# Loading an output projection in two halves of sixteen heads instead of five pieces, in a one-core decode kernel on Trainium2

## The chip, the cores and the metric

The kernel runs on one core of a Trainium2 chip. The metric is the device time of one launch in microseconds (us). A run with rounds is timed in turn with the kernel before on the same chip.

The engines in the profile: PE is TensorE's matmul, PEld its weight load, DVE is VectorE, ACT ScalarE, POOL GpSimd, and SP the SyncE engine, which issues the loads. A q behind an engine's name means its sequencer, which waits, branches and issues (PEq, SPq). L860 means line 860 of that kernel's source. A packet is one record of the DMA engines' work; in these wo loads it is one contiguous row of one partition (the 10 KB part below has 128 packets of 10,240 bytes). A load with one row per partition is thus eight packets for each of the 16 DMA engines.

## The reference

One decode step: attention of 32 query heads over 8 key/value groups with a cache of 65,536 keys, plus a feed-forward branch, both added to x.

```python
q = (x @ wq).reshape(1, 1, 32, 128).transpose(0, 2, 1, 3)
k = jnp.repeat(k_cache, 4, axis=1)          # [1, 8, 65536, 128] -> 32 heads
v = jnp.repeat(v_cache, 4, axis=1)
p = softmax(einsum("bhqd,bhkd->bhqk", q, k) * 128 ** -0.5)
o = einsum("bhqk,bhkd->bhqd", p, v)
A = o.transpose(0, 2, 1, 3).reshape(1, 1, 4096) @ wo      # wo: [4096, 512]
B = gelu(xn @ w1 + b1) @ w2 + b2            # xn = layernorm(x), also A's input
return x + A + B
```

The two caches are 268 MB of the 280.5 MB that the kernel reads. wo is 4 MB, 32 KB for each of the 128 partitions, and it is the last thing loaded.

## The kernel before

K, V and finally wo come through one queue (SP's) into one large SBUF buffer. A piece of wo goes over the place of the last but one K block. The last V block lands before wo, and while wo comes in, the last attention output is finished and weighted.

A piece of wo is loaded with contiguous rows per partition: with `(p r) n -> p r n`, partition p holds wo rows p*r to p*r + r - 1. These rows mix heads and elements, so the attention output of a piece must be spread to the same order. Before, seven groups of four heads were loaded in pieces of 16, 8 and 4 heads (4, 2 and 1 groups, WP), and spread. The eighth group was loaded head by head (1 KB rows), so its output needed no spreading.

```python
def dma_wo():
    for i, (g0, n) in enumerate(WP):              # 16, 8, 4 heads
        r = n * HPG                               # HPG = 4 heads of a group
        sch.dma(SP, lambda ...: sp.dma_start(
            out=wo_sb[:, g0 * HPG:g0 * HPG + r, :],
            in_=A_wo[g0 * HPG * DH:(g0 + n) * HPG * DH, :].rearrange("(p r) n -> p r n", r=r)),
            wsem[i], writes=[f"wo{i}"])
    for i, n in enumerate((3, 1)):                # the last group: 3 heads and 1
        ... in_=A_wo[...].rearrange("(h p) n -> p h n", p=128) ...
```

Spreading is a VectorE multiplication of the output (oT_all) by a 0/1 mask (part_m) into oM_bf. Placing is a TensorE product of oM_bf with a second mask (part_r), then a cast to oX_bf. The final sum is 32 rows of four products, each row one of a partition's 32 rows of wo:

```python
for i, (g0, n) in enumerate(WP):                  # place: three products, one cast
    sch.op(PE, lambda ...: pe.matmul(pA[:, PA_O + g0 * HPG:PA_O + g0 * HPG + r],
                                     lhsT=oM_bf[:, i, :], rhs=part_r[i][:, :], ...))
sch.op(DVX, lambda: dve.tensor_copy(out=oX_bf[:, :], in_=pA[:, PA_O:PA_O + GE * HPG]), ...)
weigh_3(GE, G, "oL")                              # the last group's output
...
for i, (g0, n) in enumerate(WP):
    for r in range(g0 * HPG, (g0 + n) * HPG):
        for kt in range(KT):                      # KT = 4 column strips
            fin_mm(kt, oX_bf[:, r:r + 1], wo_sb[:, r, kt * 128:(kt + 1) * 128], ["oX", f"wo{i}"], ...)
for h in range(HPG):                              # the last group
    ... fin_mm(kt, oT_all[...], wl_sb[:, h, ...], ["oL", f"wl{0 if h < WH[0] else 1}"], ...)
```

The kernel's outer block, with its loop over the K and V blocks, ends behind the first 64 of these products; all engines meet there.

Of the kernel before, what the change touches and what calls it, by code (L numbers as in the profile page):

```python
# [6 lines left out]
BF = mybir.dt.bfloat16  # L7
F32 = mybir.dt.float32
ACTF = mybir.ActivationFunctionType
ALU = mybir.AluOpType  # L10
AX = mybir.AxisListType
# [229 lines left out]
def bass_parallel_sum__gqa_block_cached__dense_activation_gelu__decode_kernel(  # L241
# [13 lines left out]
    D = A_x.shape[-1]  # L255
    DH = 128
    H = A_wq.shape[1] // DH
    G = A_k_cache.shape[1]
    HPG = H // G
# [3 lines left out]
    KT = D // 128  # L263
    TPF = 8
    FPU = 16
    TPD = FPU * TPF
# [20 lines left out]
    sch = _Sched(nc)  # L287
    PE = sch.add_engine("pe", "pe", is_pe=True)
    DVE = sch.add_engine("dve", "dve")
    ACT = sch.add_engine("act", "act")  # L290
    POOL = sch.add_engine("pool", "pool")
    SP = sch.add_engine("sp", "sp")
    DVX = sch.add_engine("dvx", "dvx")
# [3 lines left out]
    pe = nc.tensor  # L297
    dve = nc.vector
    act = nc.scalar
    pool = nc.gpsimd  # L300
    sp = nc.sync

    def sb(name, shape, dt):
        return nc.alloc_sbuf_tensor(name, shape, dt)

    ident_bf = sb("ident_bf", [128, 128], BF)
    ident_f = sb("ident_f", [128, 128], F32)
# [5 lines left out]
    kv = sb("kv", [128, 3 * PCOL], BF)  # L313
    at_k1 = kv_at = nc.sbuf_base - 6 * PCOL
    late = [kv_at + 40 * 1024]
    early = [at_k1 + 2 * PCOL]

    def sb_in(place, name, shape, dt):
        t = nc.alloc_sbuf_tensor_at(name, shape, dt, offset=place[0])
        n = (4 if dt == F32 else 2) * math.prod(shape[1:])  # L320
        place[0] += (n + 31) // 32 * 32
        return t
# [23 lines left out]
    w2_at = w1_at + KT * F  # L346
    w2_sb = kv[:, w2_at:w2_at + FC * D].rearrange("p (fc n) -> p fc n", fc=FC)
    GE = G - 1
    WP = []
    g0 = 0  # L350
    while g0 < GE:
        n = next(m for m in (4, 2, 1) if g0 + m <= GE)
        WP.append((g0, n))
        g0 += n
    wo_sb = kv[:, 0:GE * HPG * D].rearrange("p (r n) -> p r n", n=D)
    wl_at = TPD * DH
    wl_sb = kv[:, wl_at:wl_at + HPG * D].rearrange("p (h n) -> p h n", h=HPG)
    kt_ring = sb("kt_ring", [128, NKT * FCOL], BF)
    P_bf = [sb(f"P_bf{i}", [128, CW], BF) for i in range(2)]
    P_v = [P_bf[i][:, :].rearrange("p (t j) -> p t j", j=HPG) for i in range(2)]  # L360
# [15 lines left out]
    rden = sb_in(late, "rden", [128, H], F32)  # L376
    o_sum = sb_in(late, "o_sum", [128, H], F32)
    oT_all = sb_in(late, "oT_all", [128, H], BF)
    oX_bf = sb_in(late, "oX_bf", [128, GE * HPG], BF)
    oM_bf = sb_in(late, "oM_bf", [128, len(WP), 128], BF)  # L380
    part_m = [sb(f"part_m{i}", [128, DH // (n * HPG)], BF) for i, (_, n) in enumerate(WP)]
    part_r = [sb(f"part_r{i}", [128, n * HPG], BF) for i, (_, n) in enumerate(WP)]
    flag = sb("flag", [1, 2 * NU], BF)

    pst = [nc.alloc_psum_tensor(f"pst{i}", [128, 1024], BF) for i in range(NPT)]
# [1 line left out]
    pA = nc.alloc_psum_tensor("pA", [128, 512], F32)  # L387
    pO = nc.alloc_psum_tensor("pO", [128, 512], F32)
# [4 lines left out]
    PA_O = 64  # L393
    PA_ST = 128
    PO_SUM = HPG

    csem = [sch.dsem(f"csem{i}") for i in range(6)]
    sem_x = sch.dsem("dx")
    sem_misc = sch.dsem("dmisc")
    sem_w1 = sch.dsem("dw1")  # L400
    sem_w2 = sch.dsem("dw2")
    wsem = [sch.dsem(f"wsem{i}") for i in range(len(WP))]
    lsem = [sch.dsem(f"lsem{i}") for i in range(2)]
    sem_out = sch.dsem("dout")

    for t, res in ((ident_bf, "ident_bf"), (ident_f, "ident_f")):
# [4 lines left out]
                out=t[:, :], in_=t[:, :], compare_op=ALU.not_equal, fill=1.0,  # L411
                base=0, pattern=[[-1, 128]], channel_multiplier=1,
            ),
            reads=[res], writes=[res],
# [62 lines left out]
        sch.dma(SP, lambda: sp.dma_start(out=w2_sb, in_=B_w2.rearrange("(p fc) n -> p fc n", fc=FC)),  # L477
                sem_w2, writes=["w2"])

    WH = (HPG - 1, 1)  # L480

    def dma_wo():
        for i, (g0, n) in enumerate(WP):
            r = n * HPG
            sch.dma(SP, lambda g0=g0, n=n, r=r: sp.dma_start(
                out=wo_sb[:, g0 * HPG:g0 * HPG + r, :],
                in_=A_wo[g0 * HPG * DH:(g0 + n) * HPG * DH, :].rearrange("(p r) n -> p r n", r=r)),
                wsem[i], writes=[f"wo{i}"])
        h0 = 0
        for i, n in enumerate(WH):  # L490
            sch.dma(SP, lambda h0=h0, n=n: sp.dma_start(
                out=wl_sb[:, h0:h0 + n, :],
                in_=A_wo[(H - HPG + h0) * DH:(H - HPG + h0 + n) * DH, :].rearrange("(h p) n -> p h n", p=128)),
                lsem[i], writes=[f"wl{i}"])
            h0 += n

    dma_small()
    dma_wq()
# [262 lines left out]
    def weigh_3(a, b, res):  # L761
        cs, hs = slice(a * GW, b * GW), slice(a * HPG, b * HPG)
        sch.op(DVX, lambda: dve.tensor_tensor(out=o_c[:, cs], in0=o_all[:, cs], in1=coef[:, cs], op=ALU.mult),
               reads=["coef", "o0", "o1"], writes=["o_c"])
        sch.op(DVX, lambda: dve.tensor_reduce(out=heads(o_sum, a, b), in_=by_head(o_c, a, b), axis=AX.X,
                                              op=ALU.add), reads=["o_c"], writes=["o_sum"])
        sch.op(DVX, lambda: dve.tensor_tensor(out=oT_all[:, hs], in0=o_sum[:, hs], in1=rden[:, hs], op=ALU.mult),
               reads=["o_sum", "rden"], writes=[res])


    def spread():
        for i, (g0, n) in enumerate(WP):
            r, a = n * HPG, DH // (n * HPG)
            sch.op(DVX, lambda g0=g0, n=n, i=i, r=r, a=a: dve.tensor_tensor(
                out=oM_bf[:, i, :].rearrange("p (h a) -> p h a", a=a),
                in0=oT_all[:, g0 * HPG:g0 * HPG + r].unsqueeze(2).to_broadcast([128, r, a]),
                in1=part_m[i][:, :].unsqueeze(1).to_broadcast([128, r, a]), op=ALU.mult),
                reads=["oT", f"part_m{i}"], writes=[f"oM{i}"])


    def body(i):
        last = i == NU // 2 - 1
        for f in range(2 * FPU):
            transposes(i, f)
            if f == 1:
                load_q(i)
            if f % FPU == FPU - 1:
                done_chunk(f"K{i % 2}{'ab'[f // FPU]}")
            if f == FPU + LAG + 1:
                stats_1()  # L790
            if f == FPU + LAG + 3:
                stats_2(2 * i)
            if f in W_AT:
                weights(2 * i, W_AT.index(f))
            if f >= LAG:
                scores(f - LAG)
        for f in range(2 * FPU - LAG, 2 * FPU):
            scores(f)
        pv(2 * i, 0, 24)
        stats_1()  # L800
        pv(2 * i, 24, 48)
        stats_2(2 * i + 1)
        for j in range(HPG):
            weights(2 * i + 1, j)
        keep_max(i)
        if last:
            weigh_1()
        pv(2 * i, 48, TPD)
        pv(2 * i + 1, 0, 32)
        total(i)  # L810
        if last:
            weigh_2()
            weigh_3(0, GE, "oT")
            spread()
        pv(2 * i + 1, 32, TPD)

    W_AT = [FPU + LAG + 4 + 2 * j for j in range(HPG)]
# [10 lines left out]
        sch.reads.setdefault(res, []).append(made)  # L828
    free.update(("K1a", "K1b", "Va", "Vb"))
    issue_chunks()  # L830
    for i, (_, n) in enumerate(WP):
        r = n * HPG
        for t, res, pat in ((part_m[i], f"part_m{i}", "p (a r) -> p a r"), (part_r[i], f"part_r{i}", "p (a r) -> p r a")):
            sch.op(DVE, lambda t=t, pat=pat, r=r: dve.tensor_reduce(
                out=t[:, :], in_=ident_f[:, :].rearrange(pat, r=r), axis=AX.X, op=ALU.max),
                reads=["ident_f"], writes=[res])
    marks, marks2 = [], []
    for i in range(NU // 2):
        marks.append(len(PE.ops))
# [5 lines left out]
    marks.append(len(PE.ops))  # L845


    for i, (g0, n) in enumerate(WP):
        r = n * HPG
        sch.op(PE, lambda g0=g0, i=i, r=r: pe.matmul(  # L850
            pA[:, PA_O + g0 * HPG:PA_O + g0 * HPG + r], lhsT=oM_bf[:, i, :], rhs=part_r[i][:, :], start=True, stop=True),
            reads=[f"oM{i}", f"part_r{i}"], writes=["pA"])
    sch.op(DVX, lambda: dve.tensor_copy(out=oX_bf[:, :], in_=pA[:, PA_O:PA_O + GE * HPG]), reads=["pA"], writes=["oX"])
    weigh_3(GE, G, "oL")

    R = 0
    pR = pss[R]

    def fin_mm(kt, lhsT, rhs, reads, first, last, publish):
        sch.op(PE, lambda: pe.matmul(pR[32 * kt:32 * kt + 1, 0:128], lhsT=lhsT, rhs=rhs, start=first, stop=last),  # L860
               reads=reads, writes=[f"pss{R}"], publish=publish)

    for kt in range(KT):
        fin_mm(kt, ones_f[:, 0:1], f_rows[:, kt * 128:(kt + 1) * 128], ["f_rows", "ones_f"], True, False, kt == KT - 1)
    rest = {}
    for i, (g0, n) in enumerate(WP):
        if i == 1:
            rest.update((e, len(e.ops)) for e in (PE, DVE, SP))
        for r in range(g0 * HPG, (g0 + n) * HPG):
            for kt in range(KT):  # L870
                fin_mm(kt, oX_bf[:, r:r + 1], wo_sb[:, r, kt * 128:(kt + 1) * 128], ["oX", f"wo{i}"], False, False,
                       r == (g0 + n) * HPG - 1 and kt == KT - 1)
    for h in range(HPG):
        for kt in range(KT):
            fin_mm(kt, oT_all[:, GE * HPG + h:GE * HPG + h + 1], wl_sb[:, h, kt * 128:(kt + 1) * 128],
                   ["oL", f"wl{0 if h < WH[0] else 1}"], False, h == HPG - 1, h == HPG - 1 and kt == KT - 1)
    NR = 32 * (KT - 1) + 1
    sch.op(DVE, lambda: dve.tensor_copy(out=fin_bf[0:NR, :], in_=pR[0:NR, 0:128]),
           reads=[f"pss{R}"], writes=["fin"])
# [3 lines left out]
        sem_out, reads=["fin"], writes=["out_dram"],  # L883
# [5 lines left out]
    n = len(head)  # L889
# [61 lines left out]
```

## Time and profile before

| | before |
|---|---|
| time, median of 3 runs | 656.14 us (655.99 to 656.57) |
| span of the profiled run | 654.7 us |
| DMA packets of SP's queue (q1) | 6744 |
| granted TensorE clock, mean, and in the windows from 641 us on | 0.786, and 0.50 |
| last V block lands | 642.21 us |
| last piece of wo lands | 652.20 us |
| TensorE's last product ends | 652.61 us |

A landing is the start of the DMA's issue plus its time "from issue to landing". It is read to 0.01 us, so sums can be off by 0.01. The last column of an issue line is that time, the column before it the size. In a timeline line the columns are start, length, engine, line and operation, output and inputs, shapes, count, and in brackets the idle time just before with what ended it. The lines themselves are shown in the prediction.

### The profile page before, as it was taken

How to read it: one execution, taken by the hardware profiler on the slowest of the kernel's cores; microseconds unless marked ns; L12 is line 12 of the kernel's file. 1: busy time of each engine (PE TensorE's matmuls, PEld its weight loads, DVE VectorE, ACT ScalarE, POOL GpSimd, SP SyncE). 2: the span in 40 equal slices, each digit the busy share in tenths (PEclk: the TensorE clock that was granted, in tenths of full speed). 3: DMA queues.
4: the chain of work that ended last, by engine and by line, in shares of the span. 5: the costliest groups of instructions: out<-in, count | busy, mean ns of one | idle time of the engine just before them, and what ended most of it. 6: DMA issues, size and time to landing. Idle time of an engine off the chain costs nothing.

```text
span 654.7 us, 29020 instructions
## 1 busy us (share of the span) xinstructions
PE 532.5 (81%) x12682; PEld 506.2 (77%) x12682; DVE 281.6 (43%) x574; ACT 249.9 (38%) x454; POOL 5.6 (1%) x74
## 2 busy tenths in 40 slices
PE   2388498696969959697895969879596996998997
PEld 0187498696969959697895969879596996998996
DVE  3245063361625436162552616345261633645363
ACT  0134053351624425153451615335161543535351
POOL 0000000000000000000000000000000000000000
PEclk9789598695968869596895959679595877969695
DMA  9999999999999999999999999999999999999997
GB/s 385 444 428 438 419 447 434 436 424 444 436 424 424 444 436 428 424 444 440 420 436 433 440 424 440 424 444 432 432 420 448 436 424 428 422 454 410 432 432 303
DMA packets 6903, 280.66 MB, mean 429 GB/s; under 512 B 874, under 2 KB 1388, under 8 KB 1516
## 3 DMA queue, kind: packets, MB, share of 16 engines
q1 hardware_dynamic: 6744, 280.50, 99.4%
q8 instruction: 8, 0.13, 0.1%
q10 hardware_dynamic: 148, 0.01, 0.0%
q14 instruction: 3, 0.02, 0.0%
HBM read 280.50 MB, written 0.00 MB: 428 GB/s over the span
## 4 chain that ended last, share of the span: by engine, by line
DMA 56%; PE 33%; DVE 3%; another core or an unknown queue 3%; ACT 2%; issue 2%; SPq 1%; POOL 0%; ACTq 0%; DVEq 0%
DMA kv<-in_A_k_cache_dram 40%; PE pst L596 16%; DMA kv<-in_A_v_cache_dram 9%; DMA kv<-in_A_wo_dram 6%; PE pss L644 5%; PE pA L713 4%; PE pO L713 4%; DVE pmax L652 1%; DMA rows_bf<-in_A_x_dram 1%; PE pA L671 1%; ACT kt_ring L635 1%; PE pA L682 1%; DVE kt_ring L633 1%; PE pO L532 1%
## 5 line engine op out<-in xcount | busy, mean ns | idle before, releaser
L596 PE MATMUL pst<-ident_bf,kv 128*128 128x128 bf16 x4096 | 335.9, 233 | 85.0 <-POOL flag L453 81.9
L596 PEld LDWEIGHTS pst<-ident_bf,kv 128*128 x4096 | 262.6, 105 | 87.0 <-issue 86.9
L635 ACT ACTIVATE kt_ring<-pst 128x1024 bf16<-128x1024 bf16 x192 | 196.6, 1024 | 314.1 <-PE pst L596 299.3
L633 DVE COPY kt_ring<-pst 128x1024 bf16<-128x1024 bf16 x320 | 217.5, 691 | 221.1 <-PE pst L596 218.1
L644 PE MATMUL pss<-q_cur,kt_ring 128*128 128x4 bf16 x4096 | 174.4, 165 | 3.6 <-issue 2.0
L644 PEld LDWEIGHTS pss<-q_cur,kt_ring 128*128 128x128 bf16 x4096 | 154.2, 97 | 9.6 <-issue 5.6
L695 ACT ACTIVATE P_bf<-pss,negm 128x128 bf16<-128x128 f32 x128 | 57.2, 546 | 58.5 <-DVE negm L685 58.5
L713 PE MATMUL pO<-P_bf,kv 128*128 128x4 bf16 x2048 | 60.7, 166 | 5.8 <-issue 4.3
L713 PEld LDWEIGHTS pO<-P_bf,kv 128*128 128x128 bf16 x2048 | 56.9, 101 | 11.1 <-issue 9.1
L713 PEld LDWEIGHTS pA<-P_bf,kv 128*128 128x128 bf16 x2048 | 60.2, 106 | 4.6 <-issue 3.6
L713 PE MATMUL pA<-P_bf,kv 128*128 128x4 bf16 x2048 | 59.4, 166 | 4.4 <-issue 3.5
L695 ACT ACTIVATION_READ_ACCUMULATOR P_bf<-pss,negm 128x1 f32 x128 | 35.0, 274 | 0.0
L728 DVE COPY o_all<-pO 128x4 f32 (+1 forms) x16 | 2.6, 161 | 54.5 <-PE pO L735 54.5
L652 DVE TENSOR_REDUCE pmax<-pss 128x4 f32<-128x512 f32 x32 | 21.9, 685 | 7.2 <-PE pss L644 7.2
L728 DVE COPY o_all<-pA 128x4 f32 (+1 forms) x16 | 2.6, 161 | 38.2 <-PE pA L713 38.2
L671 PE MATMUL pA<-ident_f,pmax 128*4 128x128 f32 x64 | 13.4, 296 | 4.0 <-DVE pmax L652 2.7
L682 PE MATMUL pA<-diag,ones_f 4*128 4x4 f32 x64 | 14.2, 290 | 0.0
L673 DVE TENSOR_REDUCE gmax<-pA 4x1 f32<-4x128 f32 x32 | 8.8, 274 | 10.3 <-PE pA L671 10.3
L682 PEld LDWEIGHTS pA<-diag,ones_f 4*128 4x128 f32 x64 | 11.4, 222 | 2.0
L685 DVE TENSOR_SCALAR negm<-pA 128x4 f32<-128x4 f32 x32 | 5.2, 161 | 14.2 <-PE pA L682 14.2
L525 PE MATMUL pA<-ones_bf,xn_row 1*128 1x1 bf16 x4 | 0.3, 173 | 12.7 <-DVE xn_row L521 12.7
L525 PEld LDWEIGHTS pA<-ones_bf,xn_row 1*128 1x128 bf16 x4 | 0.2, 114 | 12.7 <-DVE xn_row L521 12.7
(80 smaller groups left out, 81.4 us busy)
## 6 DMA issues: line engine op xcount, KB each, us to landing
kv<-in_A_k_cache_dram SPq DMA_DIRECT2D x6, 4096.0 KB, 37.4
kv<-in_A_v_cache_dram SPq DMA_DIRECT2D x4, 4096.0 KB, 22.1
kv<-in_A_wq_dram SPq DMA_DIRECT2D x1, 4096.0 KB, 12.5
kv<-in_B_w_dram SPq DMA_DIRECT2D x2, 1792.0 KB, 17.9
kv<-in_A_wo_dram SPq DMA_DIRECT2D x1, 2048.0 KB, 34.5
kv<-in_A_wo_dram SPq DMA_DIRECT2D x1, 1024.0 KB, 36.6
kv<-in_A_wo_dram SPq DMA_DIRECT2D x1, 512.0 KB, 37.4
kv<-in_A_wo_dram SPq DMA_DIRECT2D x1, 384.0 KB, 37.9
```

What stands on the lines that cost most here:

```text
L532: sch.op(PE, lambda: pe.matmul(out, lhsT=lhsT, rhs=rhs, start=first, stop=last), reads=reads, writes=[res], publish=publish)
L596: ins = pe.transpose(pst[tb][:, at * 128:(at + 1) * 128], kslot[0][:, t, :], ident_bf[:, :]).ins
L633: e, fn = DVE, lambda tb=tb, dst=dst: dve.tensor_copy(out=dst, in_=pst[tb][:, :])
L635: e, fn = ACT, lambda tb=tb, dst=dst: act.activation(out=dst, in_=pst[tb][:, :], func=ACTF.Copy)
L644: lambda k=k, kb=kb, at=at, t=t: pe.matmul(pss[k][:, at:at + HPG], lhsT=kt_ring[:, kb * FCOL + t * 128:kb * FCOL + (t + 1) * 128], rhs=q_c ...
L652: lambda k=k: dve.tensor_reduce(out=pmax[:, :], in_=pss[k][:, 0:CW].rearrange("p (t j) -> p j t", j=HPG), axis=AX.X, op=ALU.max),
L671: sch.op(PE, lambda: pe.matmul(pA[0:HPG, PA_ST:PA_ST + 128], lhsT=pmax[:, 0:HPG], rhs=ident_f[:, :], start=True, stop=True), reads=["pmax" ...
L673: sch.op(DVE, lambda: dve.tensor_reduce(out=gmax4[:, :], in_=pA[0:HPG, PA_ST:PA_ST + 128], axis=AX.X, op=ALU.max), reads=["pA"], writes=[" ...
L682: sch.op(PE, lambda: pe.matmul(pA[:, PA_SB:PA_SB + HPG], lhsT=ones_f[0:HPG, 0:128], rhs=diag4[0:HPG, 0:HPG], start=True, stop=True), reads ...
L685: sch.op(DVE, lambda us=us: dve.tensor_scalar(out=negm[:, us], in0=pA[:, PA_SB:PA_SB + HPG], scalar1=-1.0, scalar2=None, op0=ALU.mult), re ...
L695: lambda: act.activation(out=P_v[k][:, :, j], in_=src[:, :, j], func=ACTF.Exp, bias=negm[:, at:at + 1], scale=1.0, accum_out=sums[:, at:at ...
L713: lambda k=k, t=t: pe.matmul(acc[:, 0:HPG], lhsT=vslot[:, k * TPD + t, :], rhs=P_v[k][:, t, :], start=t == 0, stop=t == TPD - 1),
```

## The change

The intent: cut wo in two halves of sixteen heads, with rows of 16 KB each. Half 0 comes as one load, half 1 in three parts of 10, 5 and 1 KB per partition. The large 10 KB part gives time for the output of the last group to be spread and placed like the others. There are fewer and longer rows, and one mask pair instead of three.

```diff
-    wo_sb = kv[:, 0:GE * HPG * D].rearrange("p (r n) -> p r n", n=D)
-    wl_at = TPD * DH
-    wl_sb = kv[:, wl_at:wl_at + HPG * D].rearrange("p (h n) -> p h n", h=HPG)
+    NW = 2
+    WR = H // NW
+    WA = DH // WR
+    WS = (((0, WR),), ((0, 10), (10, 15), (15, WR)))
+    wo_sb = kv[:, 0:H * D].rearrange("p (r n) -> p r n", n=D)
 (cut: tile shapes, semaphores)
+    def place(w):
+        ws = slice(w * WR, (w + 1) * WR)
+        sch.op(PE, lambda: pe.matmul(pO[:, PO_X + w * WR:PO_X + (w + 1) * WR], lhsT=oM_bf[:, w, :],
+                                     rhs=part_r[:, :], start=True, stop=True),
+               reads=[f"oM{w}", "part_r"], writes=["pO0"])
+        sch.op(DVX, lambda: dve.tensor_copy(out=oX_bf[:, ws], in_=pO[:, PO_X + w * WR:PO_X + (w + 1) * WR]),
+               reads=["pO0"], writes=[f"oX{w}"])
 (cut)
-            spread()
+            spread(0, 0, WR, "oT")
+            spread(1, 0, WR - HPG, "oT")
 (cut: six mask reductions become two)
-    for i, (g0, n) in enumerate(WP):
-        ... three placing products and one cast
+    place(0)
     weigh_3(GE, G, "oL")
+    spread(1, WR - HPG, WR, "oL")
 (cut)
+    for w in range(NW):
+        if w:
+            place(w)
+            rest = {e: len(e.ops) for e in (PE, DVE, SP)}
+        for r0, r1 in WS[w]:
+            end = w == NW - 1 and r1 == WR
+            for r in range(r0, r1):
+                for kt in range(KT):
+                    fin_mm(kt, oX_bf[:, w * WR + r:w * WR + r + 1], wo_sb[:, w * WR + r, kt * 128:(kt + 1) * 128],
+                           [f"oX{w}", f"wo{w}_{r0}"], False, end and r == WR - 1, r == r1 - 1 and kt == KT - 1)
```

More of the change, by code (lines that the diff above doesn't have):

```diff
@@ L348, in bass_parallel_sum__gqa_block_cached__dense_activation_gelu__decode_kernel @@
     GE = G - 1
-    WP = []
-    g0 = 0
-    while g0 < GE:
-        n = next(m for m in (4, 2, 1) if g0 + m <= GE)
-        WP.append((g0, n))
-        g0 += n
-    wo_sb = kv[:, 0:GE * HPG * D].rearrange("p (r n) -> p r n", n=D)
-    wl_at = TPD * DH
-    wl_sb = kv[:, wl_at:wl_at + HPG * D].rearrange("p (h n) -> p h n", h=HPG)
+    NW = 2
[3 more added lines that the diff above has]
+    wo_sb = kv[:, 0:H * D].rearrange("p (r n) -> p r n", n=D)
     kt_ring = sb("kt_ring", [128, NKT * FCOL], BF)
@@ L378, in bass_parallel_sum__gqa_block_cached__dense_activation_gelu__decode_kernel @@
     oT_all = sb_in(late, "oT_all", [128, H], BF)
-    oX_bf = sb_in(late, "oX_bf", [128, GE * HPG], BF)
-    oM_bf = sb_in(late, "oM_bf", [128, len(WP), 128], BF)
-    part_m = [sb(f"part_m{i}", [128, DH // (n * HPG)], BF) for i, (_, n) in enumerate(WP)]
-    part_r = [sb(f"part_r{i}", [128, n * HPG], BF) for i, (_, n) in enumerate(WP)]
+    oX_bf = sb_in(late, "oX_bf", [128, H], BF)
+    oM_bf = sb_in(late, "oM_bf", [128, NW, 128], BF)
+    part_m = sb("part_m", [128, WA], BF)
+    part_r = sb("part_r", [128, WR], BF)
     flag = sb("flag", [1, 2 * NU], BF)
@@ L395, in bass_parallel_sum__gqa_block_cached__dense_activation_gelu__decode_kernel @@
     PO_SUM = HPG
+    PO_X = 64
     csem = [sch.dsem(f"csem{i}") for i in range(6)]
@@ L401, in bass_parallel_sum__gqa_block_cached__dense_activation_gelu__decode_kernel @@
     sem_w2 = sch.dsem("dw2")
-    wsem = [sch.dsem(f"wsem{i}") for i in range(len(WP))]
-    lsem = [sch.dsem(f"lsem{i}") for i in range(2)]
+    wsem = [sch.dsem(f"wsem{i}") for i in range(sum(len(s) for s in WS))]
     sem_out = sch.dsem("dout")
@@ L478, in dma_w12 @@
                 sem_w2, writes=["w2"])
-    WH = (HPG - 1, 1)
     def dma_wo():
-        for i, (g0, n) in enumerate(WP):
-            r = n * HPG
-            sch.dma(SP, lambda g0=g0, n=n, r=r: sp.dma_start(
-                out=wo_sb[:, g0 * HPG:g0 * HPG + r, :],
-                in_=A_wo[g0 * HPG * DH:(g0 + n) * HPG * DH, :].rearrange("(p r) n -> p r n", r=r)),
-                wsem[i], writes=[f"wo{i}"])
-        h0 = 0
-        for i, n in enumerate(WH):
-            sch.dma(SP, lambda h0=h0, n=n: sp.dma_start(
-                out=wl_sb[:, h0:h0 + n, :],
-                in_=A_wo[(H - HPG + h0) * DH:(H - HPG + h0 + n) * DH, :].rearrange("(h p) n -> p h n", p=128)),
-                lsem[i], writes=[f"wl{i}"])
-            h0 += n
+        for i, (w, (r0, r1)) in enumerate((w, s) for w in range(NW) for s in WS[w]):
+            src = A_wo[w * WR * DH:(w + 1) * WR * DH, :].rearrange("(p r) n -> p r n", r=WR)
+            sch.dma(SP, lambda w=w, r0=r0, r1=r1, src=src: sp.dma_start(
+                out=wo_sb[:, w * WR + r0:w * WR + r1, :], in_=src[:, r0:r1, :]), wsem[i], writes=[f"wo{w}_{r0}"])
     dma_small()
@@ L768, in weigh_3, with spread @@
                reads=["o_sum", "rden"], writes=[res])
-    def spread():
-        for i, (g0, n) in enumerate(WP):
-            r, a = n * HPG, DH // (n * HPG)
-            sch.op(DVX, lambda g0=g0, n=n, i=i, r=r, a=a: dve.tensor_tensor(
-                out=oM_bf[:, i, :].rearrange("p (h a) -> p h a", a=a),
-                in0=oT_all[:, g0 * HPG:g0 * HPG + r].unsqueeze(2).to_broadcast([128, r, a]),
-                in1=part_m[i][:, :].unsqueeze(1).to_broadcast([128, r, a]), op=ALU.mult),
-                reads=["oT", f"part_m{i}"], writes=[f"oM{i}"])
+    def spread(w, h0, h1, res):
+        sch.op(DVX, lambda: dve.tensor_tensor(
+            out=oM_bf[:, w, h0 * WA:h1 * WA].rearrange("p (h a) -> p h a", a=WA),
+            in0=oT_all[:, w * WR + h0:w * WR + h1].unsqueeze(2).to_broadcast([128, h1 - h0, WA]),
+            in1=part_m[:, :].unsqueeze(1).to_broadcast([128, h1 - h0, WA]), op=ALU.mult),
+            reads=[res, "part_m"], writes=[f"oM{w}"])
+    def place(w):
[5 more added lines that the diff above has]
+               reads=["pO0"], writes=[f"oX{w}"])
     def body(i):
@@ L830, in bass_parallel_sum__gqa_block_cached__dense_activation_gelu__decode_kernel @@
     issue_chunks()
-    for i, (_, n) in enumerate(WP):
-        r = n * HPG
-        for t, res, pat in ((part_m[i], f"part_m{i}", "p (a r) -> p a r"), (part_r[i], f"part_r{i}", "p (a r) -> p r a")):
-            sch.op(DVE, lambda t=t, pat=pat, r=r: dve.tensor_reduce(
-                out=t[:, :], in_=ident_f[:, :].rearrange(pat, r=r), axis=AX.X, op=ALU.max),
-                reads=["ident_f"], writes=[res])
+    for t, res, pat in ((part_m, "part_m", "p (a r) -> p a r"), (part_r, "part_r", "p (a r) -> p r a")):
+        sch.op(DVE, lambda t=t, pat=pat: dve.tensor_reduce(
+            out=t[:, :], in_=ident_f[:, :].rearrange(pat, r=WR), axis=AX.X, op=ALU.max),
+            reads=["ident_f"], writes=[res])
     marks, marks2 = [], []
@@ L845, in bass_parallel_sum__gqa_block_cached__dense_activation_gelu__decode_kernel @@
     marks.append(len(PE.ops))
-    for i, (g0, n) in enumerate(WP):
-        r = n * HPG
-        sch.op(PE, lambda g0=g0, i=i, r=r: pe.matmul(
-            pA[:, PA_O + g0 * HPG:PA_O + g0 * HPG + r], lhsT=oM_bf[:, i, :], rhs=part_r[i][:, :], start=True, stop=True),
-            reads=[f"oM{i}", f"part_r{i}"], writes=["pA"])
-    sch.op(DVX, lambda: dve.tensor_copy(out=oX_bf[:, :], in_=pA[:, PA_O:PA_O + GE * HPG]), reads=["pA"], writes=["oX"])
+    place(0)
     weigh_3(GE, G, "oL")
+    spread(1, WR - HPG, WR, "oL")
     R = 0
@@ L864, in bass_parallel_sum__gqa_block_cached__dense_activation_gelu__decode_kernel @@
         fin_mm(kt, ones_f[:, 0:1], f_rows[:, kt * 128:(kt + 1) * 128], ["f_rows", "ones_f"], True, False, kt == KT - 1)
-    rest = {}
-    for i, (g0, n) in enumerate(WP):
-        if i == 1:
-            rest.update((e, len(e.ops)) for e in (PE, DVE, SP))
-        for r in range(g0 * HPG, (g0 + n) * HPG):
-            for kt in range(KT):
-                fin_mm(kt, oX_bf[:, r:r + 1], wo_sb[:, r, kt * 128:(kt + 1) * 128], ["oX", f"wo{i}"], False, False,
-                       r == (g0 + n) * HPG - 1 and kt == KT - 1)
-    for h in range(HPG):
-        for kt in range(KT):
-            fin_mm(kt, oT_all[:, GE * HPG + h:GE * HPG + h + 1], wl_sb[:, h, kt * 128:(kt + 1) * 128],
-                   ["oL", f"wl{0 if h < WH[0] else 1}"], False, h == HPG - 1, h == HPG - 1 and kt == KT - 1)
+    for w in range(NW):
[8 more added lines that the diff above has]
+                           [f"oX{w}", f"wo{w}_{r0}"], False, end and r == WR - 1, r == r1 - 1 and kt == KT - 1)
     NR = 32 * (KT - 1) + 1
```

## The prediction

> **What bounds the kernel now.** I read the page's per-slice table first, then the queue totals, the chain of waits from the last projection load on, the list of DMA issues, the timeline of the last microseconds, and last the trace's records of single DMA packets.
>
> ```profile
> span 654.7 us, 29020 instructions
> ...
> DMA  9999999999999999999999999999999999999997
> ...
> q1 hardware_dynamic: 6744, 280.50, 99.4%
> ```
>
> The sixteen DMA engines are busy from the first slice to the last: the kernel is a stream of 280.5 MB at 428 GB/s. Only what shortens that stream, or what follows its last byte, can move the end. TensorE is at 81%, but it runs beside the stream. The chain of waits, in order of time, shows what follows:
>
> ```profile
> 613.99 37.89 DMA kv<-in_A_wo_dram
> 651.88 0.14 issue
> 652.01 0.62 PE pss L860 x12
> 652.64 0.02 issue
> 652.66 0.29 DVE fin_bf L878
> ```
>
> The stream's last parts are pieces of wo. After the fourth lands come the last TensorE products, one VectorE copy, and the output DMA (issued at 652.98; the span ends at 654.7). That tail, from 652.66 on, is not touched by the change. The issues and their landings (columns: out<-in, queue, count, KB, us to landing):
>
> ```profile
> kv<-in_A_wo_dram SPq DMA_DIRECT2D x1, 2048.0 KB, 34.5
> kv<-in_A_wo_dram SPq DMA_DIRECT2D x1, 1024.0 KB, 36.6
> kv<-in_A_wo_dram SPq DMA_DIRECT2D x1, 512.0 KB, 37.4
> kv<-in_A_wo_dram SPq DMA_DIRECT2D x1, 384.0 KB, 37.9
> ...
> kv<-in_A_wo_dram SPq DMA_DIRECT2D x1, 128.0 KB, 37.7
> ```
>
> The timeline gives their issues at 612.56, 613.04, 613.51, 613.99 and 614.46. So they land at 647.11, 649.62, 650.89, 651.88 and 652.20: gaps of 2.51, 1.27, 0.99 and 0.33 us. TensorE in that time:
>
> ```profile
> 647.40 1.93 PE L860 MATMUL pss<-kv,oX_bf 128*1 128x128 bf16 x64
> 649.66 1.02 PE L860 MATMUL pss<-kv,oX_bf 128*1 128x128 bf16 x32 [0.33 <-PEq L897]
> 650.93 0.59 PE L860 MATMUL pss<-kv,oX_bf 128*1 128x128 bf16 x16 [0.24 <-DMA kv<-in_A_wo_dram]
> 652.01 0.60 PE L860 MATMUL pss<-kv,oT_all 128*1 128x128 bf16 x16 [0.49 <-DMA kv<-in_A_wo_dram]
> ```
>
> Each group starts just after its piece lands (0.04 us after the second and third, 0.14 after the fourth) and ends before the next: TensorE waits for the stream, not the reverse. Four products make one row of wo (one head's 1 KB of each partition). In the instruction records of a group the second row starts 0.06 us after the first and the others 0.107 us apart; the last takes 0.31 us to its end.
>
> **What the Trainium skill says.** "DMA: Bandwidth & Descriptors", section "Why a DMA increments its semaphore by 16 and not by 1": a DMA is spread over engines that finish independently, and only the full count means that all has landed. The trace agrees: the DMA share is 0.99 in 648 to 649, 0.63 in 650 to 651 and 0.21 in 651 to 652, so engines drop out over some two microseconds and the slowest sets each landing. The same page, "Why small descriptors are slow (HBM only)": each packet carries a fixed overhead, bad at 256 bytes. Here 1 KB, 4 KB, 8 KB, 14 KB and 16 KB packets take 0.046, 0.161, 0.313, 0.535 and 0.614 us: nearly proportional, with under 0.01 us of fixed cost. "TensorE: Matmul & The Clock Gate", section "Wait — 56ns, not 53.3ns?": start to start is 106.7 ns for 128 columns while the array is cold. The trace has 0.107 us between rows at a granted clock of 0.50. Four products share one interval because they go to four column strips of the array.
>
> **The change part by part.**
>
> 1. *The loads.* Before, each partition gets 16, 8, 4 and four times 1 KB; after, 16, 10, 5 and 1 KB: the same 32 KB. With eight partitions to an engine (128 over 16), an engine handles 56 packets before and 32 after. From packet durations: 10 KB lies between 8 and 14 KB at 0.037 us per KB, so 0.387; 5 KB is 0.161 + 0.037 = 0.198. Behind the common 16 KB piece, before costs 8 x (0.313 + 0.161 + 4 x 0.046) = 5.27 us and after 8 x (0.387 + 0.198 + 0.046) = 5.05. But packets overlap a little: the gaps between landings give 0.314, 0.159, 0.041 and 0.041 us per packet, that is 0.039 us per KB and almost no fixed part. By these, 10 KB is 0.391, 5 KB 0.198, and after is 8 x (0.391 + 0.198 + 0.041) = 5.04 against 5.10 before. I take the landings, which are those of the slowest engine: **the stream ends 0.06 us earlier**, with 0.2 as the most. Expected landings: 647.11, 650.24, 651.82, 652.15.
>
> 2. *Spreading and placing.* Before: three spread multiplications (0.69 us together), three placing products (0.24 us), one cast. After: spreads of 16 and 12 heads, one placing product and a cast for half 0; then, behind half 0's 64 products, the last group's spread, one more placing product and its cast. Half 0's operand should be ready near 646.9, not 647.34, as it waits for one product and 16 columns only. But half 0 lands at 647.11, so at most 0.25 us is gained there, and it is idle time. Its 16 rows then start their last product near 647.17 + 0.06 + 14 x 0.107 = 648.73.
>
> 3. *The new chain for half 1.* The last group's weighing took three VectorE operations, 647.25 to 647.83; a spread of some 0.2 us follows, so its operand is ready near 648.0, before TensorE gets there. The second placing product runs near 648.85 to 649.05, its cast to about 649.3. The program's outer block then ends: before, the first product after it started 0.33 us after the last one before it ended, so about 649.7 now. The 10 KB piece lands at 650.24. **The added round trip has some 0.5 us to spare** and costs nothing.
>
> 4. *The end of TensorE's work.* Before, the first of 4 rows started at 652.01 (0.14 after the fourth landing), and all ended at 652.61. After, 10 rows run from 650.29 to about 651.5. The five rows of the third piece start at 651.87 and the last row follows in the same beat, as its piece landed by 652.15: the sixth row starts at 651.87 + 0.06 + 4 x 0.107 = 652.36 and ends near 652.67. So **TensorE ends 0.06 us later** although the stream ends 0.06 us earlier: six rows lie behind the second-last landing in place of four, against 0.09 us saved in the wait before them.
>
> 5. *Six mask reductions become two*, at 26.0 to 27.5 us. VectorE is then idle to 33.45, and the load that waits for VectorE there is issued at 26.12, before most of them. Worth nothing.
>
> Sum: +0.06 us, and between -0.15 (if the packet durations are right) and +0.1. On 656.14 that is **656.2 us**; I put 656.1, leaning a little to the cheaper packets.
>
> **The rivals.**
>
> *A: packets matter more than I think.* The slowest engine has 24 packets fewer. If each costs more than the durations show, the end could come 0.5 us earlier, near 655.6. For it: the rate falls from 401 to 72 GB/s over the last microseconds, where the small packets lie. Against it: the DMA share falls as much, so engines are finished rather than slow, and the gap of the 1 KB piece is 0.041 us per packet.
>
> *B: the placing round trip takes the place of the waits.* If half 1's operand came after 650.24, ten rows would slide into the third piece's time and push the end. That needs a delay over 0.5 us; then each further tenth up to 0.3 us vanishes in the gap before 651.82, and only the rest counts. Even 1.2 us late would end the kernel near 656.6. Against it: the same sequence of spread, product, cast and next product takes about 0.5 us now.
>
> *C: an instruction fetch hits the slowest DMA engine.* The packet records show one of 16 KB on the instruction queue from 650.05 to 651.16, just after the block's end. It did not hold up the slowest engine here, whose gaps are regular. If it shifts to that engine or time, the end comes 0.6 to 1.1 us later, near 657. It is there in both kernels.
>
> *D: the whole stream drifts.* 0.1% of it is 0.65 us; the three runs before span 0.6 us.
>
> **Range and chances.** All that the change does is under 0.25 us in my sums; the scatter of runs and rival C are larger. So 655.5 to 656.8. Two per cent is 13 us, more than the entire tail behind the last V load, so within 2% has 0.98, and the rest is split evenly.
>
> **What would show it.** Right: q1's packets fall by 384 to 6360; gaps between the four wo landings near 3.13, 1.58 and 0.33 us; groups of 64, 40, 20 and 4 products with TensorE idle before the 40 and the 20, and none before the last 4. Step 1 is wrong if the last three gaps sum to under 4.9 us. Step 3 is wrong if the wait before the 40 products names VectorE's cast and not the DMA. Step 4 is wrong if TensorE stands idle before its last 4 products. The prediction as a whole is wrong if the span moves by over 0.7 us: then the cause must lie in the stream or the fetch, not in the products.

## The result, and the profile after

The changed kernel took 655.98 us (median of 6 runs, 655.83 to 656.67), the kernel before 655.97 us (6 runs, 655.73 to 656.57). The ratio is 1.0002, with a 95% interval from 0.9989 to 1.0015: the same. Ratios here are the mean time of one kernel's runs over that of the other's of the same rounds, so not quite the ratio of the medians. All outputs are right.

The page of the changed kernel (span, DMA share in 40 slices, SP's queue with packets, MB and share):

```profile
span 655.3 us, 29014 instructions
...
DMA  9999999999999999999999999999999999999997
...
q1 hardware_dynamic: 6344, 280.50, 99.2%
```

The stream is as full as before, with the same bytes. It has 400 packets fewer, not 384: there are also 16 packets of 4 bytes fewer, one for each of the 16 DMA engines, which fits the semaphore writes of the one load that is gone. The profiled run was the slowest of the six, at 656.67 us, which matters below. The issues of wo in it:

```profile
kv<-in_A_wo_dram SPq DMA_DIRECT2D x1, 2048.0 KB, 35.0
kv<-in_A_wo_dram SPq DMA_DIRECT2D x1, 1280.0 KB, 37.7
kv<-in_A_wo_dram SPq DMA_DIRECT2D x1, 640.0 KB, 38.7
...
kv<-in_A_wo_dram SPq DMA_DIRECT2D x1, 128.0 KB, 38.6
```

Issued at 612.67, 613.15, 613.63 and 614.10, they land at 647.72, 650.82, 652.36 and 652.69: gaps of 3.10, 1.54 and 0.33 us. Their sum is 4.97 us, where the kernel before had 5.09. TensorE in the timeline:

```profile
647.86 1.87 PE L845 MATMUL pss<-kv,oX_bf 128*1 128x128 bf16 x64
649.66 0.19 PE L765 MATMUL pO<-part_r,oM_bf 128*128 128x16 bf16 x1
650.96 1.23 PE L845 MATMUL pss<-kv,oX_bf 128*1 128x128 bf16 x40 [1.10 <-DMA kv<-in_A_wo_dram]
652.40 0.81 PE L845 MATMUL pss<-kv,oX_bf 128*1 128x128 bf16 x24 [0.21 <-DMA kv<-in_A_wo_dram]
```

The groups are 64, 40 and 24 products. The 40 wait for the DMA, not for the new placing product at 649.66. The last four products run on in the group of 24, with no idle time before them. The chain of waits ends so:

```profile
613.63 38.73 DMA kv<-in_A_wo_dram
652.36 0.04 issue
652.40 0.84 PE pss L845 x24
653.24 0.02 issue
653.26 0.29 DVE fin_bf L861
```

Before, the chain came through the last but one piece (3 heads) and the last products (12 in the chain's line, of a group of 16); now it comes through the last but one part (5 rows) and 24 products, 0.84 us in place of 0.62.

To compare traces apart from the scatter of the stream ahead of them, I count from the landing of the last V block. From there to the last wo landing it took 9.99 us before and 9.87 after; from there to TensorE's last end 0.41 before and 0.52 after. The sums are 10.40 and 10.39 us. A gain of 0.12 us in the stream went back as 0.11 us of TensorE work behind it.

### The profile page after: what moved, and what is told of

Its sections match the earlier page's. It is cut to its first block, busy times and chain, and to the rows that moved or that the text cites. A ratio compares the mean times of both kernels' runs of the same rounds, so it can differ in the third digit from the quotient of the medians.

```text
span 655.3 us, 29014 instructions
## 1 busy us (share of the span) xinstructions
PE 534.1 (82%) x12681; PEld 508.6 (78%) x12681; DVE 281.0 (43%) x571; ACT 250.0 (38%) x454; POOL 5.6 (1%) x74
## 4 chain that ended last, share of the span: by engine, by line
DMA 55%; PE 37%; issue 4%; DVE 2%; ACT 2%; SPq 1%; POOL 0%; ACTq 0%
DMA kv<-in_A_k_cache_dram 45%; PE pst L581 19%; PE pss L629 6%; DMA kv<-in_A_wo_dram 6%; PE pA L698 5%; PE pO L698 4%; DMA kv<-in_A_v_cache_dram 4%; DVE pmax L637 2%; PE pA L656 1%; PE pA L667 1%; ACT kt_ring L620 1%; DVE kt_ring L618 1%; PE pO L720 1%; ACT P_bf L680 1%; SPq L444 0%
## 5 line engine op out<-in xcount | busy, mean ns | idle before, releaser
L698 PE MATMUL pO<-P_bf,kv 128*128 128x4 bf16 x2048 | 60.6, 165 | 5.5 <-issue 4.3
L698 PEld LDWEIGHTS pO<-P_bf,kv 128*128 128x128 bf16 x2048 | 56.8, 100 | 10.0 <-issue 8.5
L698 PEld LDWEIGHTS pA<-P_bf,kv 128*128 128x128 bf16 x2048 | 60.2, 106 | 4.4 <-issue 3.1
L698 PE MATMUL pA<-P_bf,kv 128*128 128x4 bf16 x2048 | 59.3, 166 | 4.2 <-issue 3.0
```

The lines of the kernel that those rows point to most:

```text
L698: lambda k=k, t=t: pe.matmul(acc[:, 0:HPG], lhsT=vslot[:, k * TPD + t, :], rhs=P_v[k][:, t, :], start=t == 0, stop=t == TPD - 1),
```

## The experiments

Each is an edit of the changed kernel, but for `b_again`. The quoted figures of a trace are landings and instruction starts, read as above. "Tail" is the time from the last wo landing to the end of TensorE's last product.

| trace | V to last wo landing | tail | V to TensorE's end | first to last wo landing | time, median us |
|---|---|---|---|---|---|
| before | 9.99 | 0.41 | 10.40 | 5.09 | 655.97 |
| b_again | 10.03 | 0.40 | 10.43 | 5.13 | 655.78 (one run) |
| after | 9.87 | 0.52 | 10.39 | 4.97 | 655.98 |
| a_again | 9.87 | 0.55 | 10.42 | 4.98 | 656.31 |
| e1_one_piece | 9.76 | 2.01 | 11.77 | 4.86 | 657.24 |
| e2_row_pieces | 10.78 | 0.32 | 11.10 | 5.70 | 656.56 |
| e3_old_sizes | 9.92 | 0.32 | 10.24 | 5.02 | 655.59 |
| e3_again | 9.92 | 0.32 | 10.24 | 5.02 | 655.66 |
| g_10_3_2_1 | 9.91 | 0.32 | 10.23 | 5.02 | 655.75 |
| e4_late_1 | 9.87 | 0.53 | 10.40 | 4.97 | 655.85 |
| e5_late_5 | 9.85 | 3.25 | 13.10 | 4.96 | 658.50 |
| e6_more_bytes | 14.80 | 0.54 | 15.34 | 9.89 | 661.08 |

The first four (a_again, e1, e2, e3) shared 7 runs of the kernel before, with a median of 655.81 us; b_again, e4, e5 and e6 shared 7 with 655.79; e3_again and g_10_3_2_1 shared 9 with 655.75. No run is 2% from the kernel before. Four ratios to it: e1 1.0018 (1.0001 to 1.0035), e5 1.0040 (1.0024 to 1.0057) and e6 1.0082 (1.0065 to 1.0098) are clear of 1, e2 with 1.0006 (0.9990 to 1.0023) is not. The other ratios have 1 in their intervals.

### The two kernels again

No edit.

> The changed kernel once more, for a second trace. Theory (the stream sets the end, the change trades 0.1 us of stream for 0.1 us of TensorE): time within 0.6 us of 655.98; gaps between the four wo landings again near 3.10, 1.54 and 0.33 us; TensorE ends about 0.55 us after the last landing; whatever the span differs by is already there at the landing of the last V load (642.8 in the first trace). Rival (the change itself scatters): the last V load lands at the same time and the part behind it differs.

> The kernel before once more, for a second trace. Theory: from the landing of the last V load to the end of TensorE's last product it takes 10.4 us, as in its first trace (9.99 to the last wo landing and 0.41 behind it) and as in both traces of the changed kernel (10.39 and 10.42); the sum of the gaps from the first to the last wo landing is again 5.09 us against 4.97. Rival (the 0.12 us between these sums is scatter): the sum falls to 5.0 or below.

The kernel before showed 5.13 us of gaps and the changed one 4.98, so the difference of 0.12 to 0.16 us in the stream, over the two traces of each, is no scatter between traces; the sums to TensorE's end agree within 0.03 us in all four traces. The four runs of a_again reached from 655.65 to 657.22 us, so the expectation of "within 0.6 us" held for the median (656.31) alone.

b_again shows one thing more, which the first trace hides:

```profile
649.65 1.68 PE L860 MATMUL pss<-kv,oX_bf 128*1 128x128 bf16 x48 [0.33 <-PEq L897]
```

The piece of 8 heads landed at 649.38, and its products started 0.27 us later, at the block's end (PEq L897). In the first trace landing (649.62) and block's end (649.66) nearly fell together, so the start 0.04 us behind the landing was not proof of a wait for the data. It cost nothing: the next piece's products followed without a gap (48 in one line).

These traces also show where one run differs from another. In the profiled run of a_again (655.65 us) the last V block landed at 641.87, in the first trace of the changed kernel (656.67 us) at 642.82. That is 0.95 us, of a difference of 0.93 in the spans. Going back through the landings: the K block landing at 119.2 is level (119.18 and 119.25), and the V block behind it lands at 138.53 and at 139.40. That V block was issued at 112.60 in the one and 115.27 in the other, 6.6 and 4.0 us before the K block ahead of it landed. The windows of 119 to 120 and 120 to 122 us show it (columns: stretch, length, busy time of PE, PEld, DVE, ACT and POOL, clock, DMA share, GB/s), first a_again, then the first trace of the changed kernel:

```profile
119.00:120.00 1.00, 0.51 (x6) 0.52 (x7) 0.00 (x0) 0.00 (x0) 0.12 (x2) 0.50 1.06 459
120.00:122.00 2.00, 2.00 (x21) 2.00 (x20) 0.77 (x2) 0.59 (x1) 0.00 (x0) 0.50 1.13 492
```

```profile
119.00:120.00 1.00, 0.44 (x5) 0.45 (x6) 0.00 (x0) 0.00 (x0) 0.12 (x2) 0.50 0.79 328
120.00:122.00 2.00, 2.00 (x22) 2.00 (x21) 0.77 (x2) 0.52 (x1) 0.00 (x0) 0.50 0.83 360
```

The stream loses most of its 0.9 us here, with no part of the change involved. SP issues that load when products of TensorE end (SPq L444 <- PE pA L698 in the waits), and TensorE was behind. Between 40 and 85 us it stood idle, for nothing that the profile shows ("issue"), for 13.6 us in four stretches of over 2 us in the first trace of the changed kernel, and for 7.7 us in two in a_again. One of the four:

```profile
73.59 1.50 PE L698 MATMUL pO<-P_bf,kv 128*128 128x4 bf16 x51 [4.33 <-issue]
```

A 16 KB packet of the instruction queue lies in each of these six stretches. The three traces that issue that V load at 115.3 to 115.5 us (this one, e2 and e6) have such a stretch that ends at 80.5 to 80.9; in the nine others, with the load at 112.6 to 114.0, the last ends at 78.5 or earlier. That the fetches cause the stretches, and what makes them differ, was not tested.

### Half 1 in one load

```diff
-    WS = (((0, WR),), ((0, 10), (10, 15), (15, WR)))
+    WS = (((0, WR),), ((0, WR),))
```

> Half 1 of wo as one load of 16 KB rows, nothing else changed. Theory: 16 packets per DMA engine fewer but the same bytes, so the gap from the first to the second wo landing is 4.9 to 5.0 us; all 16 rows of products then lie behind the last landing, 0.045 + 0.06 + 14 x 0.107 + 0.31 = 1.9 us in place of 0.55, so about 1.3 us slower, near 657.3. Rival (packets cost much more than their durations show): the stream gains 0.3 us or more and the loss is 1 us or less. Rival (TensorE's tail is hidden anyway): no slower.

```profile
651.87 1.87 PE L845 MATMUL pss<-kv,oX_bf 128*1 128x128 bf16 x64 [2.87 <-DMA kv<-in_A_wo_dram]
```

In the timeline of this run all 64 products of half 1 wait for one landing (651.73) and end 2.01 us behind it. The stream is 0.11 us shorter than the changed kernel's (the gap is 4.86 us, just under the expected 4.9 to 5.0), the tail 1.49 us longer. The time was 657.24 us, 1.26 over the changed kernel's first median. So the products behind the last landing are on the path, all of them, and larger packets alone gain a tenth of a microsecond.

### Half 1 in rows of 1 KB

```diff
+    WS = (((0, WR),), tuple((r, r + 1) for r in range(WR)))
```

> Half 1 of wo as 16 loads of one row, so 1 KB packets throughout: 104 packets per DMA engine more than the changed kernel, plus their semaphore writes. Theory: each costs 0.003 us beyond its bytes, so the landings of half 1 are 16 x 0.33 = 5.25 us behind half 0, 0.3 us later than now, while only one row lies behind the last landing (0.36 us in place of 0.55): together +0.1 us. Rival (packets cost 0.02 us each, as would be needed for half a microsecond from the 24 packets that the change saves): +2 us.

Measured: 5.70 us from first to last landing, not 5.25, and a tail of 0.32. So the theory had the sign and the tail, but a packet costs more than twice what it said, and TensorE ended 0.70 us later (11.10 against 10.40), not 0.1. With 104 data packets per DMA engine more than the changed kernel, (5.70 - 4.97) / 104 = 0.007 us each; counted from the last V landing, (10.78 - 9.87) / 104 = 0.009. The rival's 0.02 us is out. The milder runs give the same: from one load to three parts (16 packets) 0.11 us, from those to the kernel before (24 packets, to 5.09 and 5.13) 0.12 to 0.16, so 0.005 to 0.007 each, semaphore writes included. A fixed price per load instead of per packet does not fit: these steps add two loads, one and thirteen, and would give 0.06, 0.12 to 0.16 and 0.06 us per load. The packet durations had pointed this way: a 16 KB packet takes 0.614 us, which is 0.0384 per KB, and a 1 KB packet 0.046, which leaves 0.008 us as the fixed part.

The cost is not one number even within this run. The first ten rows landed 0.37 us apart, 0.047 us per packet, at a DMA share of 1.06 (648.30 to 652.03 us). The last six gaps were 0.33 us, 0.041 per packet, at a share of 0.29, by which most engines were done. The prediction's 0.041 was read in such a last stretch.

The time was 656.56 us. One caution for this run: SP took 35.29 us to issue its 17 loads, as the first line shows; the seventh, eighth and tenth held it for 5.8, 8.5 and 14.3 us. The longer way to half 0 (5.07 us from the last V landing, 4.90 in the others) may belong to that; it was not tested.

```profile
613.31 35.29 SPq L479 DMA_DIRECT2D kv<-in_A_wo_dram  x17
```

```profile
613.99 6.95 SPq L491 DMA_DIRECT2D kv<-in_A_wo_dram  x2
```

```profile
612.03 2.33 SPq L479 DMA_DIRECT2D kv<-in_A_wo_dram  x5
```

The second line is the kernel before, whose fifth wo load held SP for 6.48 us; the third is the run with the old sizes, next, whose five loads took 0.43 us each. So it is not the number of loads that held SP. In both cases that waited, the loads of wo issued ahead came to 48 packets per DMA engine (8, 8, 8 and 24 before; six times 8 here); the five of the old sizes are 40 with the fifth.

### Half 1 in the old sizes

```diff
+    WS = (((0, WR),), ((0, 8), (8, 12), (12, 15), (15, WR)))
```

> The changed kernel with half 1 in pieces of 8, 4, 3 and 1 KB, the sizes of the kernel before, and its spread last group. This leaves only the new placing and the 3 KB rows for three of 1 KB. Theory: landing gaps 2.5, 1.25, 0.95 and 0.33 us, the sum 5.03; four rows behind the second-last landing as before, so TensorE ends 0.36 to 0.41 us after the last landing; 0.1 us faster than the changed kernel, which the times cannot resolve but the trace can. Rival (round trip of spread and placing matters): TensorE's group of 8 rows waits for VectorE's cast and not for the DMA, as the 8 KB piece lands 0.6 us sooner than the 10 KB one.

```profile
649.65 1.58 PE L845 MATMUL pss<-kv,oX_bf 128*1 128x128 bf16 x48 [0.69 <-PEq L880]
651.55 0.60 PE L845 MATMUL pss<-kv,oX_bf 128*1 128x128 bf16 x16 [0.33 <-DMA kv<-in_A_wo_dram]
```

Here half of the rival's sign appears in the timeline. The 8 KB part landed at 649.32, but its products started at 649.65, when the block's end let TensorE go on (PEq L880), not when the data came; the line names the block's end, though, and not VectorE's cast. Their 8 rows then ran straight into the next part's (48 products, as the profile merges them), and the last group started 0.04 us behind its landing. So these products started 0.33 us behind their landing, where 0.14 is usual for such a group, and it cost nothing: the next wait took it up. The gaps were 2.50, 1.27, 0.92 and 0.33 us, sum 5.02, and the tail 0.32. The sum to TensorE's end is 10.24 us, 0.15 under the changed kernel. The time was 655.59 us (655.52 to 655.61) against 655.81: in the expected direction, but the ratio 0.9992 has an interval from 0.9975 to 1.0009.

### The round trip made longer

One or five VectorE copies from PSUM (n = 1 or 5) between the second placing product and its cast:

```diff
+        for _ in range(n * w):
+            sch.op(DVX, lambda: dve.tensor_copy(out=kt_ring[:, 0:512], in_=pss[1][:, :]),
+                   reads=["pO0", "pss1"], writes=["kt0"])
         sch.op(DVX, lambda: dve.tensor_copy(out=oX_bf[:, ws], in_=pO[...]), reads=["pO0"], writes=[f"oX{w}"])
```

> One VectorE copy of 128 x 512 from a PSUM bank (such a copy of f_rows took 0.69 us before) put between the second placing product and its cast, so half 1's operand and the block's end come some 0.65 us later. Theory: the 40 products start at most 0.3 us later than 0.14 us after their piece's landing, the gap before the next piece takes that up, and the end stays: 10.4 us from the last V landing to TensorE's end, time as the changed kernel. Rival (the added round trip is on the path): 0.65 us slower, and the last 24 products no longer start at their piece's landing.

> The same with five copies, some 3.3 us (five at 0.69, less overlap). Theory: slack before the 40 products about 0.5 us, so they start 2.8 us later, all 64 rows run without a gap (0.06 + 14 x 0.107 + 0.31 = 1.87 us), and TensorE ends at about 12.7 us behind the last V landing in place of 10.4: 2.3 us slower, near 658.3. Rival (round trip hidden altogether by the stream): no slower. Rival (no slack): 3.3 us slower.

The timeline of the run with five copies, VectorE and TensorE:

```profile
649.18 3.59 DVE L769 CAST kt_ring<-pss 128x512 bf16<-128x512 f32 x5 [1.72 <-PE pO L765]
652.69 0.16 DVE L771 CAST oX_bf<-pO 128x16 bf16<-128x16 f32 x1
```

```profile
653.33 1.88 PE L848 MATMUL pss<-kv,oX_bf 128*1 128x128 bf16 x64 [4.19 <-PEq L883]
```

The cast ran at 652.69 instead of 649.18, so 3.51 us late. Without that the 40 products would have started at 650.23, 0.14 us behind their landing at 650.09; they started at 653.33, 3.10 us late. The spare time is thus 0.40 us. One copy gives about the same: the cast was 0.61 us late (649.80 against 649.19), the products started at 650.45, 0.18 later than the usual 0.14 behind the landing at 650.13, so 0.43 us was spare. With one copy nothing of it reached the end (10.40 us, 655.85 us); with five, 2.7 us did (13.10 us; 658.50 us, 2.5 over the changed kernel), more than the 2.3 expected, because five copies held the cast for 3.51 us and not 3.3, and because less time was spare than the 0.5 reckoned. The spare time is real and finite.

### More bytes

```diff
     def dma_wo():
+        sch.dma(SP, lambda: sp.dma_start(out=kv[:, 24576:24576 + WR * D].rearrange("p (r n) -> p r n", n=D),
+            in_=A_wo[0:WR * DH, :].rearrange("(p r) n -> p r n", r=WR)), sem_dup, writes=["dup"])
```

Half 0's products also wait for this copy, which nothing else uses.

> Half 0 of wo loaded a second time to a free place ahead of the real pieces: 2 MB more in the stream, 8 packets of 16 KB per DMA engine, nothing for TensorE. Theory (the stream sets the end): the last V landing to the last wo landing takes 8 x 0.614 = 4.9 us longer, and the time rises by 4.9 us to 660.9. Rival (the end is set by TensorE or by a wait that a longer stream hides): less than 4 us.

The last wo landing came 4.93 us later (14.80 against 9.87), the tail stayed at 0.54, and the time was 661.08 us, 5.10 over the changed kernel's first median and 5.29 over the kernel before in the same rounds. TensorE's last group still waits for its landing:

```profile
656.88 0.81 PE L850 MATMUL pss<-kv,oX_bf 128*1 128x128 bf16 x24 [0.22 <-DMA kv<-in_A_wo_dram]
```

The stream sets the end: what it grows by, the kernel grows by.

### A version meant to beat both

```diff
+    WS = (((0, WR),), ((0, 10), (10, 13), (13, 15), (15, WR)))
```

> The changed kernel with half 1 in 10, 3, 2 and 1 KB: the large piece that hides the round trip kept, the part behind the second-last landing cut from six rows to three. At 0.006 us per packet (the slope from one load to row pieces: 0.84 us over 120 packets, some of it semaphore writes) one load more costs 0.05 us, so the last landing comes 5.02 us behind the first; TensorE then ends 0.36 us behind it in place of 0.54. Theory: 10.25 to 10.3 us from the last V landing to TensorE's end against 10.4 in both kernels; time 0.1 to 0.15 us under both. Rival (the end piece is no matter): 10.4 us.

> Pieces of 8, 4, 3 and 1 KB once more. Theory: again 10.24 us from the last V landing to TensorE's end (5.02 of gaps, tail 0.32), with the first 8 rows started by the block's end about 0.3 us after their piece landed; time level with 10, 3, 2, 1 and 0.1 to 0.2 us under both kernels, more than an interval of these times shows. Rival (its 655.59 was luck of the run): 655.8 or more.

Both did in the trace what was expected, or slightly better: 10.23 and 10.24 us to TensorE's end, with tails of 0.32. The times, 655.75 and 655.66 us against 655.75 for the kernel before, have ratios of 0.9999 (0.9985 to 1.0012) and 1.0003 (0.9989 to 1.0016; one of its five runs was 657.03). A gain of 0.15 to 0.2 us is in all three traces of these two versions, but no timing here shows it (0.1 us or more under both kernels was expected), and I do not call either version faster.

## Why the prediction was right

The time, the range and the verdict held. The time alone tests little: the range is 1.3 us wide, and any change of a few tenths would have stayed in it. The steps are judged by the traces:

1. **The stream as the bound.** Right, and shown: 2 MB more cost 4.93 us in the stream and 5.10 us in the time.
2. **The loads, 0.06 us.** Right in sign, too small: the stream gained 0.12 to 0.16 us. The mis-sized term is the cost of a packet beyond its bytes. I had two readings, the packet durations (a gain of 0.22 us) and the gaps between landings (0.06), and chose the gaps, which I took to leave 0.039 us per KB and almost no fixed part. The runs lie between: they put the fixed part at 0.005 to 0.009 us for 1 KB to 16 KB rows, nearer to the 0.008 of the durations. One of the gaps was no guide: the 1 KB pieces land last, when most engines are done, and the run with 1 KB rows shows 0.041 us per packet there against 0.047 while the engines were busy. The 10 KB part took 3.10 us, as its duration promises (8 x 0.388), not 3.13. The packet count forecast, 6360, was 16 too high, as I had forgotten the 16 packets of 4 bytes that go with a load. (Two figures of the working are off without effect: its 5.27 is 5.26, and the DMA share that it gives for 648 to 649 us as 0.99 is 0.98 in the view.)
3. **The earlier operand for half 0.** It gained nothing, as said: those 64 products start 0.14 us behind their landing (647.72) instead of 0.29 (647.40 less 647.11), and then TensorE waits for the next part.
4. **The new round trip, "some 0.5 us to spare".** Right: 0.40 and 0.43 us by the two delay experiments. It is hidden in this kernel, but by the size of the first part, as the old sizes show, where the block's end behind it did take the wait's place. One reading of the kernel before was wrong here: that each group waited for its piece. The second group was held by the block's end, as its line says ([0.33 <-PEq L897]) and b_again confirms (0.27 us behind the landing). Nothing in the sum rests on it, as that wait lies ahead of other waits.
5. **TensorE's end, six rows behind the last but one landing.** Right in size: 0.52 and 0.55 us of tail where 0.52 (652.67 less 652.15) was worked out, against 0.41 and 0.40 before. The 40 products started 0.14 us behind their landing, not 0.05, which the gap behind them took up.
6. **The mask reductions** were put at nothing. No run isolates them; the last V landing, which is where they could show, is at 641.87 in one trace of the changed kernel and at 641.99 in one of the kernel before, which is within the scatter.
7. **The sum, +0.06 us.** Within the traces it is -0.01 (10.40 and 10.43 before, 10.39 and 10.42 after). The two halves of the trade cancel: that is why a change with 24 packets per DMA engine fewer moves nothing.
8. **The rivals.** Packets (A) count for more than my choice and for far less than A needs. The round trip (B) is hidden. The instruction fetch (C) is in the packet records of all traces, with its last packet starting between 649.87 and 656.13 us, and like gaps between wo landings agree within 0.05 us from trace to trace, wherever it falls; a hit on the slowest engine, 0.6 us or more by my estimate, was not seen, which does not rule it out. The drift of the stream (D) is the scatter: 0.95 us between two traces of the same kernel, all of it before the last V landing.

## What to carry to other kernels

In a kernel like this one, which ends behind a full DMA stream, the end is the last landing plus the work that depends on the last pieces: split the final load so that each piece's work fits in the time that the next piece takes to land, and keep the last two pieces small. Count both sides of such a split, the packets that it adds (here 0.005 to 0.009 us each per DMA engine, in rows of 1 KB and more) and the rows of work that it takes from behind the last landing (here 0.107 us each). When the expected effect is a tenth of the scatter, measure it inside the trace from a landmark behind the scatter, here the last V landing, and do not claim it from the times.

## What the Trainium skill lacked or had wrong

- "DMA: Bandwidth & Descriptors", "Why small descriptors are slow (HBM only)", works its per-packet overhead out for 256 bytes and says that packetization is worth it up to that size. It gives no measured cost on this chip for rows of 1 KB and more: 0.005 to 0.009 us per packet and DMA engine here (1 KB in 0.046 us, 16 KB in 0.614).
- The same page does not say how much SP's queue takes before the issue itself waits. Here 17 loads behind a full stream took 35.29 us to issue, and before the change the fifth wo load held SP for 6.48 us where the others took 0.43. In both, 48 packets of wo per DMA engine were ahead; five loads with 40 in all took 0.43 us each. The limit itself was not measured.
- No page that I read gives the time from a landing to the first product that waits for it. Here it was 0.04 us where only the data was new, and 0.13 to 0.14 us for the group whose operand was new as well and which had no other wait ahead (652.01, 650.96 and 649.99 in the traces of before, after and a_again; 0.09 for half 0 in e6). That the second wait is the cause was not tested.
- "Runtime: NRT & Kernel Launch", "Instruction fetch mechanics", gives no time for a fetch. Its 16 KB packet took 0.97 to 1.11 us in the two first traces, a data packet of that size 0.614; and idle stretches of TensorE of 2.6 to 4.3 us each held one (see "The two kernels again"; that the fetch is the cause was not tested).
